# First expert chosen earlier, its w1 pieces spaced wider, and four row buffers, in a fused attention and expert kernel

## The chip, the cores and the metric

The kernel runs on one core of one Trainium2 chip. The metric is the device time of one execution in microseconds; lower is better. Engines are named as in the profile: PE (matrix multiply), PEld (its weight loads), DVE (vector), ACT (scalar), POOL (GpSimd), SP (the engine that only issues DMAs here).

## The reference

Attention over 4 batches, 8 heads, 768 tokens of 64 numbers, where a query sees only keys in the same hash bucket, and then a mixture of 8 experts in which each token goes to one expert:

```python
mask = q_bucket[:, :, :, None] == k_bucket[:, :, None, :]
scores = np.where(mask, scale * (q @ k.T), -1e9)
attn = softmax(scores);  x = (attn @ v)        # 3072 tokens x 512
e_idx = np.argmax(x @ w_gate, axis=1)
for e in range(8):
    rows = e_idx == e
    h = np.maximum(x[rows] @ w1[e], 0.0)       # 512 -> 1024
    out[rows] = gate_w * eom * (h @ w2[e])     # 1024 -> 512
```

## The kernel before

**Attention.** 16 pairs of heads, 12 steps each, 192 steps in all; a step is 128 queries against 768 keys. `scores(s)` multiplies on PE into `ps_s` (two buffers) and DVE moves the result to `sc` (L532). `soft(s)` takes the exponential on ACT (L540). `normal(s)` runs at every even step for the two steps before: DVE finishes the row sums (`rsum`, L547, L548) and POOL scales `sc` (L550). `transposed(s)` follows four steps after `scores(s)`: PE transposes (L561) and ACT copies the result to `pts` (L562). `weighted` multiplies by V (L572) into `ps_a`. Between pairs, `spread` copies the next pair's operands across partitions with DMAs issued by SP (L503 to L511).

**Work put into the steps.** `plan(step, fn)` hangs a function on a step; it is written into every engine's program there. PE, DVE, ACT and POOL run their programs in the order written; SP's order comes from the framework's scheduler. Batch b's routing is planned in the steps of the next batch: `best`, `choose`, `prefix`, `ranks` (step 144 + 20 for the third batch), `columns`, `hot`, `table`, `entries` (step 144 + 29). The last batch's routing comes after step 195 with the first expert's first product between its parts.

**The first expert.** It is chosen by load after three batches. `pick` (planned at `late`) finds it on DVE and SP reads its number (L757). `early_gather` fetches its first 256 rows from `x_dram`, an indirect DMA on POOL (L253) into `xg`. `early_turn(a)` transposes 128 of them. `early_load(cc)` loads one of the four 512 KB pieces of its w1 into `w_raw` (two buffers), and `early_w1(cc)` splits the piece into a high and a low part on POOL (L174, L177: two operations on 128 x 1024). After the last step `w2_piece(..., "hl")` does the same with the four pieces of w2, in the same two buffers. `fill(f)` are the eight blocks of the first product, `low()` the DVE operation that belongs to each (L322).

**After attention.** `gid0` holds the first expert's first 256 rows over all four batches; `gather` fetches them (`xg`, at most `EARLY` = 2 buffers). `order()` sorts the experts, `indices` makes the row numbers `gid` and `sid`. Then the early rows' second product runs (`down_rows`, in blocks of two f), and `turn` transposes the two gathered chunks between its blocks. Then come the experts in order, r = 0 to 7. `up` is a first product in pairs of f into `ps_s`, followed by `hh` on ACT (L321) and `hl` on DVE (L322). For r = 0 the next expert's rows are gathered inside the loop over `fp` and transposed where `TURN_UP` and `TURN_DOWN` say (chunks 0 and 1 after fp = 2, chunk 2 after fp = 3, chunk 3 in the second product). Later experts' rows come in quarters by `gather_part` (L285). `send` scales a finished chunk on ACT into `yo` (L327, two buffers) and stores it by an indirect DMA on POOL (L328).

Of the kernel before, what the change touches and what calls it, by code (L numbers as in the profile page):

```python
# [8 lines left out]
F32 = mybir.dt.float32  # L9
# [10 lines left out]
B, H, S, D = 4, 8, 768, 64  # L20
# [4 lines left out]
DM = H * D  # L25
E = 8
F = 1024
NTOK = B * S
NTT = NTOK // P
CH = P  # L30
NCH = 4
# [4 lines left out]
EARLY = 2  # L36
# [17 lines left out]
def f32(ap):  # L54
    return ap.bitcast(F32)
# [3 lines left out]
def lsh_attention_then_moe(  # L59
# [120 lines left out]
    def w1_load(r, cc):  # L180
        return load_weights([P, F], w1[bass.ds(expert[r], 1), :, cc].rearrange("e p f -> p (e f)"))

    def w1_split(pool, raw, idle=""):
        return split_weights(pool, "w1", NCC, [P, F], raw, idle)
# [47 lines left out]
    gp = ctx.enter_context(tc.tile_pool(name="gp", bufs=1))  # L232
# [8 lines left out]
    def indices(pool, tacc):  # L241
        gid = pool.tile([CH, E, NCH], U32, name="gid")
        nc.vector.tensor_copy(gid, tacc[:, 0])
        sk = pool.tile([CH, E, NCH], F32, name="sk")
        nc.vector.tensor_scalar(sk, tacc[:, 2], -SKIP, SKIP, ALU.mult, ALU.add)
        sid = pool.tile([CH, E, NCH], U32, name="sid")
        nc.vector.tensor_tensor(sid, sk, tacc[:, 0], ALU.add)
        return gid, sid

    def gather(idx, n=CH, ntok=NTOK, pool=gp, bufs=EARLY):  # L250

        xg = pool.tile([CH, DM], F32, name="xg", bufs=bufs)
        nc.gpsimd.indirect_dma_start(out=xg[0:n], out_offset=None, in_=x_dram[0:ntok, :],  # L253
                                     in_offset=bass.IndirectOffsetOnAxis(ap=idx[0:n], axis=0))
        return xg, n

    def new_x0():
        return [gp.tile([P, NCC, CAP0], F32R, name=n) for n in ("xh0", "xlo0")]

    def turn(xgn, xs, c0, early=False):  # L260

        xg, n = xgn
        px = (ps_m if early else ps_t).tile([P, NCC, CH], F32, name="ps_m" if early else "ps_t")
        for cc in range(NCC):
            nc.tensor.transpose(px[:, cc, 0:n], xg[0:n].rearrange("n (p b) -> n b p", b=NCC)[:, cc], ident[0:n, 0:n])
        xh, xlo = (x[:, :, c0:c0 + n] for x in xs)
        nc.scalar.copy(xh, px[:, :, 0:n])
        nc.vector.tensor_tensor(xlo, px[:, :, 0:n], f32(xh), ALU.subtract)
# [32 lines left out]
    def new_h():  # L301
        return [ep.tile([P, NFB, CAP], F32R, name=n) for n in ("hh", "hl")]
# [20 lines left out]

    def send(r, a, n, py, sid):

        yo = mp.tile([CH, DM], F32, name="yo", bufs=2)
        nc.scalar.activation(yo[0:n], py[0:n], AF.Copy, scale=tacc[0:n, 1, r, a:a + 1])  # L327
        nc.gpsimd.indirect_dma_start(  # L328
            out=out[:, :], out_offset=bass.IndirectOffsetOnAxis(ap=sid[0:n, r, a:a + 1], axis=0),
            in_=yo[0:n], in_offset=None, bounds_check=NTOK - 1, oob_is_err=False)  # L330
# [36 lines left out]
    with ExitStack() as actx:  # L367
# [16 lines left out]
        def plan(step, *fns):  # L384
            at.setdefault(step, []).extend(fns)
# [350 lines left out]
        for b in range(B - 1):  # L736
            r = routing(b)
# [7 lines left out]
        r = routing(B - 1)  # L745
# [5 lines left out]

        late = 12 * (H // 2) * (B - 1) + 29

        def load_expert(idi, i):
            expert.append(nc.values_load(idi[0:1, i:i + 1], engines=(mybir.EngineType.SP,), min_val=0, max_val=E - 1))  # L757
# [61 lines left out]
        def early_turn(a):  # L819
            if a == 0:  # L820
                early["x"] = new_x0()
            turn(early["xg"][a], early["x"], a * CH, True)

        def early_load(cc):
            early.setdefault("raw", []).append(w1_load(0, cc))

        def early_w1(cc):
            early.setdefault("w1", []).append(w1_split(wpool, early["raw"][cc], "hl"))

        plan(late, pick)  # L830
        plan(late + 2, early_gather)
        for a in range(EARLY):
            plan(late + 6 + 2 * a, lambda a=a: early_turn(a))
        for cc in range(NCC):
            plan(late + 9 + 3 * cc, lambda cc=cc: early_w1(cc))
            plan(late + (3 + cc if cc < 2 else 3 + 3 * cc), lambda cc=cc: early_load(cc))

        with tc.manual_schedule(engines=MANUAL):
            load(0)
# [86 lines left out]
    mp = ctx.enter_context(tc.tile_pool(name="mp", bufs=1, reuse_waits="tile"))  # L926
    with tc.manual_schedule(engines=MANUAL):
        xg = [gather(gid0[:, a:a + 1]) for a in range(EARLY)]
        order()
        gid, sid = indices(mp, tacc)  # L930
        x0 = new_x0()
        for c in range(EARLY):
            py = ps_s.tile([P, 2, 512], F32, name="ps_s")[:, 0]
            for f in range(0, NFB, 2):
                down_rows(c, CH, w2s, hs, py, [f, f + 1])
                if c and f < 2 * EARLY:
                    turn(xg[f // 2], x0, f // 2 * CH)
            send(0, c, CH, py, sid)
        hs = new_h()
        w1s = early["w1"]  # L940
        xs = x0
        back = None
        xgs = {}
        parts = []
        for r in range(E):
            n = CAPS[r] if r else CAP0
            ch = chunks(r)
            nxt = chunks(r + 1) if r + 1 < E else []
            if r:
                hs = new_h()  # L950
                w2s = []
            xn, w1n, splits = new_x() if nxt else None, [], []

            def fetch(a, e):

                if e < E and a < len(chunks(e)):
                    n = chunks(e)[a]
                    for k in range((n + 31) // 32):
                        parts.append((e, a, n, k))

            def gather_some(m):
                for e, a, n, k in parts[:m]:
                    if k == 0:
                        xgs[e, a] = mp.tile([P, DM], F32, name="xq", bufs=NCH), n
                    gather_part(xgs[e, a][0], idx[:, k, e, a:a + 1], k)
                del parts[:m]

            def turned(a):
                if a < len(nxt):
                    if r == 0:  # L970
                        turn(xgs.pop((r + 1, a)), xn, a * CH)
                        return fetch(a, r + 2)
                    while any(p[:2] == (r + 1, a) for p in parts):
                        gather_some(1)
                    splits.append((a, turn_blocks(xgs.pop((r + 1, a)), xn, a * CH)))

            def split():
                while splits:
                    a, fn = splits.pop(0)
                    fn()  # L980
                    fetch(a, r + 2)

            def next_w1(cc):
                if nxt:
                    w1n.append(w1_piece(wpool, r + 1, cc))

            for fp in range(NFB // 2):
                up(w1s, xs, hs, [2 * fp, 2 * fp + 1], n)()
                if r and fp < 2:
                    w2s += w2_piece(ep, r, 4 * fp) + w2_piece(ep, r, 4 * fp + 2)  # L990
                if back is not None:
                    pch = chunks(r - 1)
                    if fp < len(pch):
                        turn_back(r - 1, fp, pch[fp], back, sid)
                if r == 0 and fp == 1:
                    idx = slot_rows(tacc)
                split()
                gather_some(2)
                for a in TURN_UP.get(fp, ()):
                    turned(a)  # L1000
                if r == 0 and fp % 2 == 0:
                    for a in (fp, fp + 1):
                        if a < len(nxt):
                            xgs[1, a] = gather(gid[:, 1, a:a + 1])[0], nxt[a]

            def hook(a, cc):
                split()
                gather_some(2)
                if a is not None:
                    turned(a)  # L1010
                if cc is not None:
                    next_w1(cc)

            hooks = [lambda i=i: hook(*i) for i in TURN_DOWN]

            def between():
                if hooks:
                    hooks.pop(0)()

            if n > 3 * CH:  # L1020
                back = [mp.tile([P, 2, CAP], F32, name="yt", bufs=2) for _ in range(NCC // 2)]
                for dp in range(NCC // 2):
                    down(w2s, hs, n, back, dp, between)
            else:
                back = None
                c0 = 0 if r else EARLY
                for a in range(c0, len(ch)):
                    all_rows(r, a, a - c0, ch[a], w2s, hs, sid, between)
            split()
            if nxt:  # L1030
                w1s, xs = w1n, xn
# [98 lines left out]
```

## Time and profile before

| | |
|---|---|
| time before | 796.67 us, median of 3 runs (796.37 to 797.16) |
| the profiled execution | 791.77 us, of which the span from first to last instruction is 790.0 us |
| busy PE, PEld | 770.3 us (98%), 608.1 us (77%) |
| busy DVE, ACT, POOL | 479.7 us (61%), 459.1 us (58%), 382.1 us (48%) |
| granted clock | 0.995 on average |

The profile is one execution. Rows of the timeline give the start in us, the duration in us, the engine, the line, the operation and the tiles; in brackets stands the idle time of the engine before the row and what ended it. Rows of the waits give the waiting engine and tile, what it waited for, and the total us, the number of times and the longest. A row of the windows gives a stretch, its length, the busy us of each engine with the number of instructions, the granted PE clock, and the DMA engines' share and GB/s. The attention steps end at about 463 us, the last batch's routing at about 488 us, and the expert loop runs from about 499 us to the end.

### The profile page before, as it was taken

Reading aid. Unit: us, or ns where it says so; the run is one execution under the profiler, and the core shown is the slowest. Engines: PE = TensorE matmul, PEld = TensorE weight load, DVE = VectorE, ACT = ScalarE, POOL = GpSimd, SP = SyncE. Lnnn points to the kernel's source line nnn. Section 1 sums busy time; section 2 is a strip of 40 time slices with the busy share of each in tenths; the row PEclk is TensorE's granted clock in tenths of the full one; section 3 lists DMA queues with packets and bytes.
Section 4 is the critical chain, followed back from the end, with each engine's and each line's share of the span. In section 5 each row is a group of like instructions: output and inputs, shape, how many; then the busy total and the mean of one; then the engine's idle time right before and its main releaser. Section 6 shows DMA issues by size and latency. Waiting matters only on the chain. (4 is left out here: it accounts for less than half of the span.)

```text
span 790.0 us, 13715 instructions
## 1 busy us (share of the span) xinstructions
PE 770.3 (98%) x4690; PEld 608.1 (77%) x4690; DVE 479.7 (61%) x1032; ACT 459.1 (58%) x934; POOL 382.1 (48%) x422
## 2 busy tenths in 40 slices
PE   7999999999999999999999999999999999999997
PEld 6777676667676767676767658878999999988895
DVE  6676667796766896675896737236363636454640
ACT  6877777777777777777768721234151525353331
POOL 7555544444543444544445892372627273746201
PEclk9999999999999999999999999999999999999999
DMA  5554454464565456455456152363444444445601
GB/s 170 135 135 88 101 128 86 118 140 85 120 145 130 81 126 143 91 123 129 88 123 166 54 137 62 106 217 124 144 147 150 152 150 148 150 150 179 220 24 39
DMA packets 84800, 98.90 MB, mean 125 GB/s; under 512 B 57999, under 2 KB 59439, under 8 KB 84720
## 3 DMA queue, kind: packets, MB, share of 16 engines
q1 hardware_dynamic: 79376, 84.58, 41.1%
q0 software_dynamic: 5200, 13.31, 5.1%
q8 instruction: 40, 0.66, 0.3%
q14 instruction: 40, 0.33, 0.1%
q10 hardware_dynamic: 144, 0.02, 0.0%
HBM read 59.49 MB, written 13.11 MB: 92 GB/s over the span
## 5 line engine op out<-in xcount | busy, mean ns | idle before, releaser
L550 POOL TENSOR_SCALAR sc<-sc,rsum 128x768 f32<-128x768 f32 x192 | 178.9, 945 | 218.1 <-DVE rsum L548 85.8
L532 DVE TENSOR_SCALAR_CACHE_REDUCE sc<-ps_s 128x768 f32<-128x768 f32 x192 | 183.3, 955 | 96.4 <-PE ps_s L528 88.4
L562 ACT COPY pts<-ps_t 128x384 f32<-128x384 f32 x384 | 164.4, 481 | 95.5 <-PE ps_t L561 95.0
L540 ACT ACTIVATE sc<-sc,mn 128x768 f32<-128x768 f32 x192 | 181.4, 945 | 15.2 <-DVE sc L532 14.3
L561 PE MATMUL ps_t<-ident,sc 128*128 128x128 f32 x1152 | 158.4, 273 | 3.9 <-POOL sc L550 1.8
L561 PEld LDWEIGHTS ps_t<-ident,sc 128*128 128x128 f32 x1152 | 137.2, 141 | 14.3 <-POOL sc L550 4.6
L572 PE MATMUL ps_a<-pts,vt 128*64 128x384 f32 x768 | 144.8, 499 | 0.0
L528 PE MATMUL ps_s<-xr,xl 128*128 128x384 f32 x384 | 117.1, 386 | 2.4 <-POOL xl L476 2.2
L528 PEld LDWEIGHTS ps_s<-xr,xl 128*128 128x128 f32 x384 | 57.9, 190 | 71.0 <-issue 33.6
L528 PE MATMUL ps_s<-yr,yl 76*128 76x384 f32 x384 | 100.0, 341 | 0.6 <-POOL yr L438 0.5
L322 DVE SCALAR_TENSOR_TENSOR hl<-ps_s,hh 128x256 fp32r<-128x256 f32 (+8 forms) x40 | 34.0, 849 | 109.0 <-ACT hh L321 88.3
L311 PE MATMUL ps_s<-xh,w1h 128*128 128x256 f32 (+7 forms) x288 | 97.8, 340 | 2.2 <-DVE hl L322 2.1
L311 PE MATMUL ps_s<-xh,w1l 128*128 128x256 f32 (+7 forms) x288 | 96.2, 334 | 0.8 <-DVE w1l L177 0.5
L311 PE MATMUL ps_s<-xlo,w1h 128*128 128x256 f32 (+7 forms) x288 | 96.0, 333 | 0.0
L285 POOL DMA_INDIRECT xq<-x_dram,idx x75 | 82.5, 1099 | 21.6 <-issue 21.1
L328 POOL DMA_INDIRECT out_dram<-yo,sid x29 | 30.6, 1056 | 116.4 <-ACT yo L327 69.2
L572 PEld LDWEIGHTS ps_a<-pts,vt 128*64 128x64 f32 x768 | 46.7, 136 | 50.4 <-issue 47.7
L321 ACT ACTIVATE hh<-ps_s 128x256 fp32r<-128x256 f32 (+8 forms) x40 | 29.1, 727 | 90.4 <-PE ps_s L311 75.6
L528 PEld LDWEIGHTS ps_s<-yr,yl 76*128 76x128 f32 x384 | 70.4, 190 | 1.2 <-POOL yr L438 1.2
L311 PEld LDWEIGHTS ps_s<-xh,w1h 128*128 128x128 f32 x288 | 54.9, 191 | 5.8 <-DVE hl L322 3.0
L311 PEld LDWEIGHTS ps_s<-xh,w1l 128*128 128x128 f32 x288 | 54.8, 190 | 2.6 <-DVE w1l L177 0.9
L311 PEld LDWEIGHTS ps_s<-xlo,w1h 128*128 128x128 f32 x288 | 54.9, 190 | 1.1
(204 smaller groups left out, 1020.6 us busy)
## 6 DMA issues: line engine op xcount, KB each, us to landing
w_raw<-in_w_dram SPq DMA_DIRECT2D x36, 512.0 KB
qk<-in_qkT_dram SPq DMA_DIRECT2D x32, 384.0 KB
xh<-in_w_dram SPq DMA_DIRECT2D x14, 512.0 KB
xlo<-in_w_dram SPq DMA_DIRECT2D x14, 512.0 KB
vt<-in_v_dram SPq DMA_DIRECT2D x16, 384.0 KB
xr<-xl SPq DMA_DIRECT2D x30, 192.0 KB
yr<-xl SPq DMA_DIRECT2D x30, 192.0 KB
xr<-yl SPq DMA_DIRECT2D x30, 192.0 KB
```

The lines of the kernel that those rows point to most:

```text
L285: nc.gpsimd.indirect_dma_start(out=xq[:, k * P:(k + 1) * P], out_offset=None, in_=x_dram.rearrange("n (a f) -> (n a) f", a=NB32), in_offse ...
L311: nc.tensor.matmul(ps, l, r, start=first and k == 0, stop=last and k == len(pairs) - 1)
L321: nc.scalar.activation(hh, ph, AF.Relu)
L322: return lambda: nc.vector.scalar_tensor_tensor(hl, ph, 0.0, f32(hh), ALU.max, ALU.subtract)
L328: nc.gpsimd.indirect_dma_start(out=out[:, :], out_offset=bass.IndirectOffsetOnAxis(ap=sid[0:n, r, a:a + 1], axis=0), in_=yo[0:n], in_offse ...
L528: nc.tensor.matmul(ss[:, n, 0:HS], l[0:k, qs], r[0:k, n * HS:(n + 1) * HS], start=first, stop=not first)
L532: nc.vector.tensor_scalar(sc, ss[:, :, 0:HS], MASKED, None, ALU.min, ALU.min, accum_out=mn)
L540: nc.scalar.activation(pr, pr, AF.Exp, bias=mn, scale=-1.0, accum_out=sums[s // GROUP][:, k:k + 1])
L550: nc.gpsimd.tensor_scalar(live[s0 + k], live[s0 + k], rs[:, k:k + 1], 0.0, ALU.mult, ALU.add)
L561: nc.tensor.transpose(tr[:, c], pr[:, (3 * h + c) * P:(3 * h + c + 1) * P], ident)
L562: nc.scalar.copy(pts[:, 3 * h:3 * h + 3, t * P:(t + 1) * P], tr)
L572: nc.tensor.matmul(st["av"][j * D:(j + 1) * D], st["v"][:, j, c], blocks[hb][j][:, c], start=(c == 0), stop=(c == NT - 1))
```

## The change

Four edits.

1. `late` goes from step 173 to step 167, so `pick` stands three steps after `ranks` of the third batch. `early_gather` and the two `early_turn` keep their steps (175, 179, 181). The four `early_w1` go from steps 182, 185, 188, 191 to 176, 180, 184, 188; the four `early_load` from 176, 177, 182, 185 to 170, 171, 177, 181.
2. `xg` gets `NCH` = 4 buffers and `yo` gets 4.
3. The second expert's first two chunks (`xg1`) are gathered right after `indices`, and its other two at fp = 0; before, two were gathered at fp = 0 and two at fp = 2.
4. In the early rows' second product, the two `turn` stand after the blocks f = 2 and f = 4 of the second chunk, not after f = 0 and f = 2.

```diff
-    def gather(idx, n=CH, ntok=NTOK, pool=gp, bufs=EARLY):
+    def gather(idx, n=CH, ntok=NTOK, pool=gp, bufs=NCH):
...
-        yo = mp.tile([CH, DM], F32, name="yo", bufs=2)
+        yo = mp.tile([CH, DM], F32, name="yo", bufs=4)
...
-        late = 12 * (H // 2) * (B - 1) + 29
+        late = 12 * (H // 2) * (B - 1) + 23
...
         plan(late, pick)
-        plan(late + 2, early_gather)
+        plan(late + 8, early_gather)
         for a in range(EARLY):
-            plan(late + 6 + 2 * a, lambda a=a: early_turn(a))
+            plan(late + 12 + 2 * a, lambda a=a: early_turn(a))
         for cc in range(NCC):
-            plan(late + 9 + 3 * cc, lambda cc=cc: early_w1(cc))
-            plan(late + (3 + cc if cc < 2 else 3 + 3 * cc), lambda cc=cc: early_load(cc))
+            plan(late + 9 + 4 * cc, lambda cc=cc: early_w1(cc))
+            plan(late + (3 + cc if cc < 2 else 2 + 4 * cc), lambda cc=cc: early_load(cc))
...
         gid, sid = indices(mp, tacc)
+        xg1 = [gather(gid[:, 1, a:a + 1]) for a in range(EARLY)]
...
-                if c and f < 2 * EARLY:
-                    turn(xg[f // 2], x0, f // 2 * CH)
+                if c and f in (2, 4):
+                    turn(xg[f // 2 - 1], x0, (f // 2 - 1) * CH)
...
-                if r == 0 and fp % 2 == 0:
-                    for a in (fp, fp + 1):
-                        if a < len(nxt):
-                            xgs[1, a] = gather(gid[:, 1, a:a + 1])[0], nxt[a]
+                if r == 0 and fp == 0:
+                    for a in range(len(nxt)):
+                        xgs[1, a] = (xg1[a] if a < EARLY else gather(gid[:, 1, a:a + 1]))[0], nxt[a]
```

## The prediction

> **What bounds the kernel now.** I read the page first, then who PE waited for, then the timelines around each of those waits, and the windows for the clock.
>
> ```profile
> span 790.0 us, 13715 instructions
> PE 770.3 (98%) x4690; PEld 608.1 (77%) x4690; DVE 479.7 (61%) x1032; ACT 459.1 (58%) x934; POOL 382.1 (48%) x422
> ```
>
> PE is busy for all but 19.7 us, so only what makes PE wait, or run slowly, can move the time. The change touches nothing before step 167 (about 397 us). Between 402 and 455 us the list of PE's waits is empty; the next two lists, for 456 to 530 us and for 530 us to the end, are the whole field of the change.
>
> ```profile
> PE ps_t L561 <- POOL sc L550: 1.5, 2, 1.2
> PE ps_t L265 <- DMA xg<-x_dram,gid: 1.3, 3, 0.5
> PE ps_m L673 <- DVE ohb L649: 1.3, 1, 1.3
> PE ps_s L311 <- DVE w1l L177: 0.5, 1, 0.5
> PE ps_s L311 <- DVE hl L322: 0.4, 1, 0.4
> ...
> PE ps_s L311 <- DVE hl L322: 1.7, 1, 1.7
> ```
>
> Six groups of waits, 6.7 us. One more loss does not show as a wait:
>
> ```profile
> 475.40:478.90 3.50, 1.73 (x19) 1.59 (x19) 3.29 (x17) 0.38 (x1) 0.32 (x1) 1.00 0.17 26
> 478.90:482.30 3.40, 3.40 (x18) 3.40 (x17) 2.75 (x17) 0.74 (x2) 0.00 (x0) 0.50 0.23 34
> ```
>
> After a stretch in which PE worked 1.73 us of 3.50, its granted clock is 0.50 for 3.4 us. PE counts as fully busy there and does half the work.
>
> **The change part by part.**
>
> *Last attention steps: gain 1.5.* The wait of 1.5 us on `sc` falls on the last pair of steps:
>
> ```profile
> 455.52 1.05 POOL L174 TENSOR_SCALAR w1h<-w_raw 128x1024 fp32r<-128x1024 f32 x1
> 458.99 1.81 POOL L550 TENSOR_SCALAR sc<-sc,rsum 128x768 f32<-128x768 f32 x2
> ```
>
> The fourth w1 split (step 191) runs from 455.52 to 458.99 and the last scaling waits behind it. After the change the fourth split is at step 188, the place that the third has now, and POOL is free when the row sums come (about 456). The scaling then starts some 3 us earlier and PE's two waits go: 1.5 us.
>
> *The one-hot of the last batch: gain 1.3.*
>
> ```profile
> 473.33 2.39 POOL L177 TENSOR_TENSOR w2l<-w_raw,w2h 128x1024 fp32r<-128x1024 f32 x1
> 473.56 2.21 DVE L642 TENSOR_SCALAR eq<-df 128x48 f32<-128x48 f32 x1
> 476.77 0.20 PE L673 MATMUL ps_m<-ohb,tri 128*128 128x48 bf16 x1 [1.33 <-DVE ohb L649]
> ```
>
> L642 works on 48 numbers and took 2.21 us: it ended with the last w2 split of POOL (473.33 + 2.39 = 475.72). So POOL holds DVE, DVE holds `ohb`, and PE stood 1.33 us. After the change the w2 splits begin 3 us earlier (POOL is free, and w_raw's buffers too, since w1's last two splits come earlier), while PE and DVE arrive 1.5 us earlier. The last split would end at about 472.7 (475.72 - 3); L642 would start at 472.05 (473.56 - 1.5) and end at 472.8 instead of 475.77. `ohb` comes 0.9 us after L642 today, so at about 473.7; PE, which began to stand at 475.44 (476.77 - 1.33), is then done at 473.9. Bounds: 0 if the w2 loads hold the splits back, 1.3 if not; I take 1.3.
>
> *The half clock: gain 1.5.* With those 1.3 us of idle time gone, PE works about 3 of the 3.5 us in which it worked 1.73. I expect no drop. Half of 3.4 us is 1.7; I take 1.5, since PE was not limited by its clock in all of it. The lower end is 0.
>
> *The gathered rows: gain 2.1, less 0.1.* A turn that waits costs more than its idle time, since PE's weight loads start anew. One turn in the early rows' second product did not wait and the next did:
>
> ```profile
> 492.88 0.40 PE L311 MATMUL ps_s<-w2h,hl 128*128 128x512 f32 x1
> 493.50 0.48 PE L311 MATMUL ps_s<-w2h,hh 128*128 128x512 f32 x1
> 494.75 0.39 PE L311 MATMUL ps_s<-w2h,hl 128*128 128x512 f32 x1
> 496.06 0.48 PE L311 MATMUL ps_s<-w2h,hh 128*128 128x512 f32 x1
> ```
>
> From the product before to the product after it is 0.62 us in the first case and 1.31 in the second: 0.7 us lost per late gather. There are three (1.3 us of idle time in the list): this one and chunks 2 and 3 of the second expert, whose gathers wait today for the turns of chunks 0 and 1. With four buffers the last two are fetched at fp = 0, two products of `up` sooner; the first pair of turns moves back by one block (493.50 to 494.75 plus one product, 1.5 us) against an idle time of at most 0.5. So 3 x 0.7 = 2.1. In return only one block now lies between the second turn and `up`, which needs its low part; I put 0.1 us on that. The two gathers put ahead of `send` on POOL delay the first store by the time of two gathers; nobody waits for those with four `yo` buffers.
>
> *The output rows: gain 1.8.*
>
> ```profile
> 721.93 1.03 POOL L328 DMA_INDIRECT out_dram<-yo,sid  x1 [0.30 <-issue]
> 724.81 0.69 ACT L327 ACTIVATE yo<-ps_m,tacc 128x512 f32<-128x512 f32 x1 [12.13 <-DMA out_dram<-yo,sid]
> 725.18 0.33 PE L311 MATMUL ps_s<-xh,w1l 128*128 128x368 f32 x1
> 727.18 0.44 PE L311 MATMUL ps_s<-xh,w1h 128*128 128x368 f32 x1 [1.67 <-DVE hl L322]
> ```
>
> ACT stood 12 us for a `yo` buffer whose store left POOL late; behind it on ACT stood `hh`, behind that `hl`, and PE missed its third `up` block. With four buffers this `yo` takes one whose store is long done, and ACT is in time. From 725.18 to 727.18 instead of about 0.2: 1.8 us.
>
> *The splits that move into steps 176 and 180: cost 0.9.*
>
> ```profile
> 420.27 1.79 POOL L550 TENSOR_SCALAR sc<-sc,rsum 128x768 f32<-128x768 f32 x2
> 424.07 1.80 POOL L550 TENSOR_SCALAR sc<-sc,rsum 128x768 f32<-128x768 f32 x2 [2.01 <-DVE rsum L548]
> 428.53 0.82 PE L561 MATMUL ps_t<-ident,sc 128*128 128x128 f32 x6
> 435.49 1.05 POOL L174 TENSOR_SCALAR w1h<-w_raw 128x1024 fp32r<-128x1024 f32 x1
> 439.43 1.79 POOL L550 TENSOR_SCALAR sc<-sc,rsum 128x768 f32<-128x768 f32 x2 [0.42 <-DVE rsum L548]
> ```
>
> Today a split sets the next scaling 3.94 us after the split's start (435.49 to 439.43). Put behind the scaling of 420.27, it moves that of 424.07 to 426.0 (420.27 + 1.79 + 3.94); its second half is ready at 427.8, and PE wants it at 428.53: 0.7 us to spare. But the split also holds DVE, so `sc` and ACT come later, and the early turns of steps 179 and 181 add an ACT and a DVE operation in just these steps. By hand I get PE late by 0.3 at step 181 and 0.6 at step 184. Ends: 0 (three splits run today without a PE wait) and 3.0 (the fourth cost 1.5, and two splits are in question). I take 0.9, nearer the three.
>
> *`pick` at step 167: 0.*
>
> ```profile
> 401.09 0.94 DVE L532 TENSOR_SCALAR_CACHE_REDUCE sc<-ps_s 128x768 f32<-128x768 f32 x1
> 404.11 0.62 PE L528 MATMUL ps_s<-xr,xl 128*128 128x384 f32 x2
> 412.85 0.16 DVE L761 SCALAR_TENSOR_TENSOR o_key<-base,expi 128x8 f32<-128x8 f32 x1
> 413.98 0.16 DVE L770 SCALAR_TENSOR_TENSOR base<-lead,base 128x8 f32<-128x8 f32 x1
> ```
>
> `pick` takes DVE 1.3 us (412.85 to 414.14) and moves into a stretch where DVE is behind. The scores that reuse the buffer freed at 402.03 start at 404.11, so 2.1 us cover 1.3. The w1 loads and SP's read of the number move with it; see the last rival.
>
> Sum: 1.5 + 1.3 + 1.5 + 2.1 + 1.8 - 0.1 - 0.9 = 7.2 us. The profiled execution would go from 791.77 to 784.6. The median of the runs is 4.9 us above that execution; I take the same 7.2 off it: **789.5 us**, 0.9% faster.
>
> **The rivals.**
>
> *The half clock stays (791.0).* The waits go, but the clock drops all the same, because the small products around 477 us do not count as work or because the drop's place is free against the kernel. For it: 0.4 us of idle time on `hl` stays there. Against it: one drop, and right behind the one stretch where PE worked under half. 789.5 + 1.5. [...]
>
> *The moved splits stall PE at full price (791.6).* Two times 1.5 instead of 0.9. Against it: the empty list from 402 to 455 us with three splits in it.
>
> *A late signal goes too (788.7).*
>
> ```profile
> 519.81 0.39 PE L311 MATMUL ps_m<-w2h,hl 128*128 128x512 f32 x1
> 525.04 0.69 ACT L327 ACTIVATE yo<-ps_m,tacc 128x512 f32<-128x512 f32 x1 [6.35 <-issue]
> 527.98 0.48 PE L311 MATMUL ps_s<-xh,w1l 128*128 128x464 f32 x1 [0.52 <-DVE w1l L177]
> ```
>
> ACT took this `yo` 4.8 us after its product ended, with no releaser shown; w1's last splits stand behind it, and PE waits for them (0.5). If it is the `yo` buffer after all, four buffers win another 0.8 (0.5 idle, at the 0.7 lost for some 0.43 idle seen above). If it is not, nothing: my value, as no DMA is named.
>
> *Slower: w1's third load gets ahead of the last copies on SP (800).*
>
> ```profile
> 416.41 0.53 SPq L503 DMA_DIRECT2D xr<-xl  x1
> 422.73 0.71 SPq L511 DMA_DIRECT2D yl<-bt  x1
> 427.74 0.60 PE L528 MATMUL ps_s<-xr,xl 128*128 128x384 f32 x2
> 453.37 0.33 SPq L167 DMA_DIRECT2D w_raw<-in_w_dram  x1
> 454.99 3.33 SPq L591 DMA_DIRECT2D x_dram<-xb  x4
> ```
>
> The third load must wait for the first split, which now ends at about 425.5 (422.06, and the 3.47 us from 455.52 to 458.99). SP's order is not the written one: at 453.37 it issued a w2 load ahead of copies to `x_dram` that are written before it. If that load stands ahead of the last pair's copies (416.41 to 423.44, 7.0 us), they run from 425.5 to 432.5, and with the same 4.3 us between the end of the copies and the scores these start at 436.8 instead of 427.74: 9.1 us lost, which outweighs 7.2, and a half clock of 1.5 behind so long a gap, 800.1 in all. It decides from 8.8 us of loss on (7.2 and the 1.6 of 0.2%). Against it: the copies are written at steps 172 and 174, the load at 177, and the first two loads followed the copies today.
>
> **How the numbers follow.** Forecast 789.5: 0.52. Half clock stays, 791.0: 0.16. Splits at full price, 791.6: 0.12. Late signal goes too, 788.7: 0.10. Slower, 800: 0.05. Little is left because new waits take the place of the old ones, within 796.67 +/- 1.6: 0.05. Chances: faster by over 0.2% (about the least that a measurement of this kernel can tell from no change; 1.6 us) 0.90, within 0.2% 0.05, slower 0.05. The range takes the late signal with the splits at no cost (789.5 - 0.8 - 0.9 = 787.8), and above the half clock and the full price of the splits together (789.5 + 1.5 + 2.1 = 793.1).
>
> **What would show it.** Right: no PE wait on `sc` L550 after 456 us, L642 under 1 us or at least `ohb` not waited for, granted clock 1.00 around 479 us, no PE wait on `xg`, no ACT wait on a store at the sixth expert. Wrong: PE waits between 420 and 440 us on `sc` or `pts`, a gap before the last pair's scores, a clock of 0.50 somewhere after 400 us, or a new wait of `up` on the low part of the first rows.

## The result and the profile after

| | before | after |
|---|---|---|
| first comparison, median | 796.67 us (796.37 to 797.16, 3 runs) | 784.27 us (782.71 to 784.55, 3 runs) |
| ratio | | 0.9866 (0.9835 to 0.9897) |
| the profiled execution, its span | 791.77 us, 790.0 us | 784.55 us, 782.8 us |
| on one later chip, median | 789.69 us (788.54 to 790.24, 9 runs) | 784.21 us (783.16 to 784.6, 5 runs) |
| ratio there | | 0.993 (0.9916 to 0.9943) |

The change makes the kernel faster, by 12.4 us in the first comparison and by 5.5 us when both ran again on another chip. The changed kernel takes the same time in both; it is the kernel before that differs by 7 us. The span of the two profiled executions fell by exactly the 7.2 us of the sum, 790.0 to 782.8, and the forecast of the time, 789.5, was 5.2 us too high, outside its range.

The head of the page of the changed kernel:

```profile
span 782.8 us, 13716 instructions
...
PE 767.5 (98%) x4690; PEld 606.8 (78%) x4690; DVE 476.8 (61%) x1032; ACT 458.6 (59%) x934; POOL 380.5 (49%) x422
```

Who PE waited for, first from 390 to 455 us, then from 455 to 530 us; from 530 us to the end its list is empty:

```profile
PE ps_t L561 <- ACT pts L562: 0.4, 1, 0.4
PE ps_t L561 <- POOL sc L550: 0.2, 1, 0.2
...
PE ps_a L311 <- issue: 1.1, 1, 1.1
PE ps_s L311 <- DVE eq L642: 0.8, 1, 0.8
PE ps_t L265 <- DMA xg<-x_dram,gid: 0.4, 1, 0.4
PE ps_t L561 <- issue: 0.3, 1, 0.3
```

The waits on `ohb`, `hl` and `w1l` are gone, those on `sc` and `xg` are down to 0.2 and 0.4 us (the prediction had none left on `xg`). New are the wait on `eq` and two rows called "issue", times for which the profile shows no releaser. The wait on `pts` is in the kernel before as well. The timeline around them (the idle time and its end in brackets):

```profile
436.57 0.87 PE L561 MATMUL ps_t<-ident,sc 128*128 128x128 f32 x6 [0.15 <-POOL sc L550]
456.37 1.79 POOL L550 TENSOR_SCALAR sc<-sc,rsum 128x768 f32<-128x768 f32 x2 [0.57 <-PE ps_t L561]
470.51 2.38 POOL L177 TENSOR_TENSOR w2l<-w_raw,w2h 128x1024 fp32r<-128x1024 f32 x1
471.67 1.28 DVE L634 TENSOR_TENSOR df<-lgt,mx 128x48 f32<-128x48 f32 x1
473.21 0.17 DVE L642 TENSOR_SCALAR eq<-df 128x48 f32<-128x48 f32 x1
473.44 0.36 PE L311 MATMUL ps_s<-xh,w1h 128*128 128x256 f32 x1 [0.78 <-DVE eq L642]
515.33 0.59 ACT L267 CAST xh<-ps_t 128x512 fp32r<-128x512 f32 x1 [2.93 <-remote]
517.41 0.40 PE L311 MATMUL ps_a<-w2l,hh 128*128 128x512 f32 x1 [1.07 <-issue]
712.08 0.69 ACT L327 ACTIVATE yo<-ps_m,tacc 128x512 f32<-128x512 f32 x1 [4.87 <-PE ps_m L311]
```

The last scaling starts at 456.37 instead of 458.99. L642, which had taken 2.21 us, takes 0.17. But POOL's last split now overlaps L634, two DVE operations earlier: it takes 1.28 us and ends at 472.95, with the split (470.51 + 2.38 = 472.89). The `hl` behind it is late and PE stands 0.78 us. ACT's `yo` of the sixth expert waits for its product and for no store.

The windows over the place of the half clock (length, busy us of PE, PEld, DVE, ACT and POOL, granted clock, DMA share, GB/s):

```profile
471.57:474.98 3.41, 2.63 (x24) 2.41 (x23) 3.24 (x10) 0.67 (x3) 1.32 (x1) 1.00 0.00 0
474.98:478.39 3.41, 3.41 (x35) 3.40 (x35) 3.24 (x23) 0.83 (x3) 0.00 (x0) 1.00 0.40 58
```

To say where the time went, I divided each profiled execution at the same PE instructions of the program (named here by their start in the trace of the kernel before) and took the us between them:

```
from - to (us)   398-437 437-461 461-474 474-477 477-482 482-500 500-505 505-513 513-540 719-729  398-784
                 splits  last sc hl, eq  ohb     clock   1st xg          2nd xg          yo
before             39.45   23.66   12.86    2.95    5.52   17.05    5.32    8.15   26.96    9.99   386.00
after              39.81   22.33   13.56    1.47    3.50   17.53    5.34    7.40   25.60    8.05   378.70
e1_same            39.45   23.65   12.75    2.95    5.56   17.05    5.32    8.14   24.38    9.79   383.14
e2_schedule        39.78   22.33   13.26    1.46    3.50   18.60    5.31    8.17   24.38   10.08   380.98
e3_yo              39.45   23.64   12.87    2.95    4.04   17.69    5.31    8.14   24.41    8.05   380.68
e4_gather          39.45   23.65   12.65    2.95    5.56   17.90    5.36    7.40   24.38    9.67   383.09
e5_after           39.81   22.33   14.21    1.47    3.50   17.92    5.34    7.40   24.38    8.05   378.51
e6_last_high       39.83   22.34   13.29    1.46    3.50   17.24    5.53    7.40   24.38    8.05   377.14
e7_no_steps        39.45   23.63   12.49    2.96    5.53   16.85    5.67    7.40   24.38    8.05   380.53
e8_turns_back      39.77   22.33   13.35    1.46    3.51   18.16    5.32    7.40   24.38    8.05   377.82
e9_xg1_late        39.84   22.34   13.52    1.46    3.50   17.39    5.31    7.40   24.38    8.05   377.30
e10_both           39.82   22.33   13.47    1.47    3.50   16.87    5.13    7.40   24.38    8.05   376.51
e11_before_last    39.45   23.66   12.94    2.60    4.27   17.72    5.32    8.23   25.17    9.93   383.38
```

The two stretches left out, 540 to 719 and 729 to 784, take 179.04 and 55.07 us in every one of them. (The first 397 us, which the change does not touch, vary by up to 1.4 us between executions.)

### The profile page after: what moved, and what is told of

The parts are those of the page before. It is cut to its first block, busy times and chain, and to the rows that moved or that the text cites. A ratio compares the mean times of both kernels' runs of the same rounds, so it can differ in the third digit from the quotient of the medians.

```text
span 782.8 us, 13716 instructions
## 1 busy us (share of the span) xinstructions
PE 767.5 (98%) x4690; PEld 606.8 (78%) x4690; DVE 476.8 (61%) x1032; ACT 458.6 (59%) x934; POOL 380.5 (49%) x422
```

## The experiments

The theory after the first comparison: the sum's mechanisms hold, and what the forecast missed is the 4.9 us that the runs of the kernel before lay above its own profile, a level of those runs. The rival: those 4.9 us are waits of the kernel that the change also takes away. The runs e1 to e4 shared one chip, where the kernel before took 789.59 us (787.79 to 792.03, 29 runs); e5 to e8 a second, with 789.69 us; e9 to e11 a third, with 789.76 us (788.01 to 793.24, 17 runs).

**e1_same**: the kernel before, unchanged.

> The kernel before, unchanged, once more. The forecast took the same 7.2 us off a median that stands 4.9 us above the profiled execution, and the result came out another 5.2 us lower. Theory 1 (the 4.9 us were something outside the kernel's waits, tied to those executions): the median now lies near the profiled 791.8 us, and between single executions stand steps of about 1.5 to 1.8 us, one half-clock stretch more or less. Theory 2 (this kernel usually loses about 5 us more than its profiled execution shows, to waits that the change removes): the median is again 796 to 797 us, and the profile shows, in an execution of that length, which waits these are.

Measured: 789.3 us (788.21 to 791.6), ratio 0.9999 (0.9986 to 1.0011). In 55 further executions of the kernel before on three chips none came near 796.37, the lowest of the first comparison. So 796.67 is a level of those three runs and not of the kernel. What raised it is not shown, nor why the changed kernel, 784.27 us in the same comparison, did not have it. Of its 12 executions the profiled one was the fastest (788.21). The late `yo` that the prediction found at 525.04 us is not there: 24.38 us from 513 to 540, against 26.96. Of this difference 1.9 us are the late `yo`; the other 0.66 are the wait on the last gathered chunk (515.31 us in the kernel before, 0.40 us), which is not there either, nor in e2 and e3.

**e2_schedule**: the first edit alone.

```diff
-        late = 12 * (H // 2) * (B - 1) + 29
+        late = 12 * (H // 2) * (B - 1) + 23
... with the steps of early_gather, early_turn, early_w1 and early_load as in the change
```

> Edit 1 alone (pick at step 167, splits at 176, 180, 184, 188). From the two traces: 3.6 to 3.9 us shorter span by the first expert's second product (wait on the last scaling 1.3 of 1.5, one-hot and its two DVE waits 1.0, half clock 1.5). Theory 1: 0.995 to 0.996 of before. Theory 2, if the hidden 5 us lie in the attention part: 0.989.

Measured: 786.45 us, ratio 0.996 (0.9944 to 0.9977), 3.1 us; the sum had 1.5 + 1.3 + 1.5 - 0.9 = 3.4 for this edit. PE's waits in this profile show what it costs:

```profile
PE ps_t L265 <- DMA xg<-x_dram,gid: 2.2, 2, 1.7
...
PE ps_s L311 <- DVE eq L642: 0.5, 1, 0.5
```

PE arrives earlier at the gathered rows, and they do not come earlier by as much: 18.60 us from 482 to 500 instead of 17.05. The second gather goes out as far ahead of PE as in e1 (5.3 us), but takes 7.0 us from its issue to its landing, where it took 5.7 in e1.

**e3_yo**: four output buffers alone.

```diff
-        yo = mp.tile([CH, DM], F32, name="yo", bufs=2)
+        yo = mp.tile([CH, DM], F32, name="yo", bufs=4)
```

> Edit 2's yo buffers alone (four for two). Theory 1: 1.8 us by the wait before the sixth expert's third block, 0.9977; with the late signal of the third yo, if that was the buffer, another 0.8 to 1.9, 0.9955. Theory 2, if the hidden 5 us are stores that leave late: 0.991 or less.

Measured: 786.98 us, ratio 0.997 (0.9958 to 0.9981), 2.4 us by the ratio. The stretch from 719 to 729 falls from 9.79 to 8.05: 1.74 us, where the sum had 1.8. The half clock is also absent in this profile, though the wait on `ohb` is there (1.3 us); the section on the hardware comes back to that.

**e4_gather**: four `xg` buffers, `xg1` and the later turns, without the rest.

```diff
-    def gather(idx, n=CH, ntok=NTOK, pool=gp, bufs=EARLY):
+    def gather(idx, n=CH, ntok=NTOK, pool=gp, bufs=NCH):
...
+        xg1 = [gather(gid[:, 1, a:a + 1]) for a in range(EARLY)]
...
-                if c and f < 2 * EARLY:
-                    turn(xg[f // 2], x0, f // 2 * CH)
+                if c and f in (2, 4):
+                    turn(xg[f // 2 - 1], x0, (f // 2 - 1) * CH)
... with the gathers at fp = 0 as in the change
```

> Edits 3 and 4 with four xg buffers, alone. Theory 1: the turns of the second expert's chunks 2 and 3 no longer wait, 1.3 us, and the first pair's wait stays or goes (0 to 0.7): 0.9975 to 0.9985. Theory 2, if the hidden 5 us are gathers that land late: 0.992 or less.

Measured: 788.12 us, ratio 0.9975 (0.9963 to 0.9988), 2.0 us by the ratio and 1.5 by the medians. Its profile does not show where they come from: 383.09 us from 398 to 784 against 383.14 in e1. The table shows two effects that cancel: chunks 2 and 3 gain 0.74 us (8.14 to 7.40), while the first two chunks lose 0.85 (17.05 to 17.90), although their turns come a block later. The second of them is late:

```profile
494.59 0.63 PE L265 MATMUL ps_t<-ident,xg 128*128 128x128 f32 x4
497.73 0.75 PE L265 MATMUL ps_t<-ident,xg 128*128 128x128 f32 x4 [1.12 <-DMA xg<-x_dram,gid]
```

**e5_after**: the changed kernel.

> The changed kernel itself, beside the kernel before on one chip. Theory 1 (the three parts add up, and the 796.67 us of the first comparison was a level of those executions): ratio 0.9905, the product of 0.996, 0.997 and 0.9975, so about 782 us where the kernel before takes 789.5. Rival (the parts help one another, and the first comparison had the right size): 0.9866, about 779 us. The late signal of PE between 511 and 518 us, seen in the first profile of the changed kernel, should be absent if it belongs to those executions, and present if the back-to-back gathers on POOL cause it.

Measured: 784.21 us, ratio 0.993 (0.9916 to 0.9943). The rival's 0.9866 is out, so the first comparison overstated the change. But the parts add up to 0.9905, and the whole gives less. PE's longest waits in this profile are that on `eq`, which was 0.5 us in e2, and that on `xg`, which was 2.2 us in e2 and 1.1 in e4:

```profile
PE ps_s L311 <- DVE eq L642: 1.4, 1, 1.4
PE ps_t L265 <- DMA xg<-x_dram,gid: 0.8, 1, 0.8
```

```profile
471.49 2.38 POOL L177 TENSOR_TENSOR w2l<-w_raw,w2h 128x1024 fp32r<-128x1024 f32 x1
471.77 0.20 DVE L632 TENSOR_REDUCE mx<-lgt 128x6 f32<-128x48 f32 x1
472.01 1.92 DVE L634 TENSOR_TENSOR df<-lgt,mx 128x48 f32<-128x48 f32 x1
474.41 0.36 PE L311 MATMUL ps_s<-xh,w1h 128*128 128x256 f32 x1 [1.43 <-DVE eq L642]
```

L634 ends at 473.93, the split at 473.87. How long it is held differs between executions: the wait on `eq` is 0.8 us in the first profile of the same kernel and 0.6 and 0.7 in e8 and e9, whose edits do not touch it. The shortfall of 0.0025 has an interval of about 0.0027 to either side, so that the parts add up is not excluded. The late signal of 515 us is absent (24.38 us from 513 to 540), so the gathers on POOL, which are the same, do not cause it by themselves.

**e6_last_high**: the changed kernel with the last w2 piece's high part on ACT.

```diff
-                w2s += w2_piece(ep, 0, f, "hl")
+                w2s += w2_piece(ep, 0, f, "l" if f == NFB - 2 else "hl")
```

> The changed kernel with the high part of the last w2 piece made on ACT, which idles there from 464.4 to 470.6 us, instead of on POOL. Theory: POOL's last split (470.51 to 472.89) holds DVE's L634, hl stands behind it, and PE waits 0.8 us on it; with 1.05 us less work on POOL the split ends about 1 us sooner and the wait goes: 0.7 us faster than the changed kernel, a tenth of a per cent. Rival: the piece's load lands no sooner than POOL came to it (about 469.3), then ACT and POOL gain nothing and hh of ACT, queued behind the copy, may come later: no change or 0.3 us slower.

Measured: 783.05 us (782.49 to 783.44), ratio 0.9917 (0.9904 to 0.9931), 1.2 us below e5 on the same chip.

```profile
469.90 1.05 ACT L176 CAST w2h<-w_raw 128x1024 fp32r<-128x1024 f32 x1 [4.68 <-DMA w_raw<-in_w_dram]
471.03 2.39 POOL L177 TENSOR_TENSOR w2l<-w_raw,w2h 128x1024 fp32r<-128x1024 f32 x1 [1.06 <-ACT w2h L176]
472.46 1.02 DVE L634 TENSOR_TENSOR df<-lgt,mx 128x48 f32<-128x48 f32 x1
473.96 0.35 PE L311 MATMUL ps_s<-xh,w1h 128*128 128x256 f32 x1 [0.56 <-DVE eq L642]
```

L634 again ends with the split (473.48 and 473.42). The wait is 0.56 us, against 1.43 in e5. That does not show a gain: e8, without this edit, has the same 0.56,

```profile
473.67 0.36 PE L311 MATMUL ps_s<-xh,w1h 128*128 128x256 f32 x1 [0.56 <-DVE eq L642]
```

and e10, with it, has 0.69 against 0.73 in e9. ACT had to wait for the load, as the rival had it. A further 0.7 us against e5 in the table (17.92 to 17.24) are gathered rows that came sooner here; nothing in this edit moves them. So the traces do not say what the timed 1.2 us are.

**e7_no_steps**: the changed kernel without its first edit.

```diff
-        late = 12 * (H // 2) * (B - 1) + 23
+        late = 12 * (H // 2) * (B - 1) + 29
... with the steps of the kernel before
```

> The changed kernel without its first edit: the steps of pick, loads, splits, gathers and turns are those of the kernel before; the gathers and the four output buffers stay. If the parts add up: 0.9945 of the kernel before, 3.2 us slower than the changed kernel, with the waits on sc (1.5) and ohb (1.3) back in the list. Rival (the steps are worth less beside the others, since the new wait on eq takes 0.8 back): 2 us slower or less.

Measured: 785.63 us, ratio 0.9953 (0.9939 to 0.9966): the product of e3 and e4, 0.9945, lies within it. So nothing speaks against the other two parts adding up, and the new steps bring 1.4 us on top of them (1.9 by the means, with an interval of about 0.9 to either side), where alone they brought 3.1. That is the rival's size. By the table between e7 and e5: `sc` 1.30, `ohb` 1.49 and the clock 2.03 are won, and 0.33 between 500 and 505; the splits 0.36, `eq` 1.72 and the first gathered pair 1.07 are lost. The half clock is in this profile:

```profile
475.09:478.50 3.41, 1.62 (x19) 1.31 (x18) 3.20 (x16) 0.38 (x1) 0.53 (x1) 1.00 0.10 15
478.50:481.91 3.41, 3.41 (x19) 3.41 (x18) 3.09 (x17) 0.38 (x1) 0.00 (x0) 0.50 0.30 45
```

**e8_turns_back**: the changed kernel with the two early turns where they were.

```diff
-                if c and f in (2, 4):
-                    turn(xg[f // 2 - 1], x0, (f // 2 - 1) * CH)
+                if c and f < 2 * EARLY:
+                    turn(xg[f // 2], x0, f // 2 * CH)
```

> The changed kernel with the turns of the first two gathered chunks at f = 0 and 2 again, as in the kernel before, instead of 2 and 4. Theory: the first gather lands as late against PE as before, so the one wait on xg of 0.4 us grows by about the block of 1.5 us that lies between: 1.5 us slower than the changed kernel, 0.2 per cent. Rival (the prediction's step: a late turn costs 0.7 us, however late): 0.7 us slower. A second rival: the list of the changed kernel shows its wait at the second turn; then nothing changes.

Measured: 783.95 us, ratio 0.9936 (0.9922 to 0.9949): no difference from e5. The wait is longer, and the stretch costs 0.24 us more (18.16 against 17.92):

```profile
493.04 0.75 PE L265 MATMUL ps_t<-ident,xg 128*128 128x128 f32 x4 [1.30 <-DMA xg<-x_dram,gid]
```

It is the second turn that waits, as the second rival had it; the first chunk is there in time at either place. The time rules out the 1.5 us (the means differ by 0.3, with an interval of about 0.8 to either side), but not the 0.7. Nor is the stretch a clean test, as the second gather took 7.5 us from issue to landing in e5 and 6.6 here.

**e9_xg1_late**: the changed kernel with the gathers of `xg1` behind the first store.

```diff
-        xg1 = [gather(gid[:, 1, a:a + 1]) for a in range(EARLY)]
...
             send(0, c, CH, py, sid)
+            if c == 0:
+                xg1 = [gather(gid[:, 1, a:a + 1]) for a in range(EARLY)]
```

> The changed kernel with the two gathers xg1 issued on POOL after the first send instead of ahead of it. Theory: the second early gather lands late (PE waits 0.83 us on xg in the changed kernel, 0.42 at that place in the kernel before) because two more gathers now share the DMA engines with it and with two w1 loads; with xg1 later the stage from the first down product to the last turn takes 7.5 us instead of 8.1, about 0.5 us off the whole (less than the interval, so the stage decides). Rival: the w1 loads on SP fill the DMA engines alone; the wait stays at 0.8.

```profile
489.40 1.03 POOL L328 DMA_INDIRECT out_dram<-yo,sid  x1 [2.11 <-ACT yo L327]
490.74 0.98 POOL L253 DMA_INDIRECT xg<-x_dram,gid  x1 [0.30 <-issue]
493.41 0.75 PE L265 MATMUL ps_t<-ident,xg 128*128 128x128 f32 x4 [0.37 <-DMA xg<-x_dram,gid]
```

Measured: 782.95 us, ratio 0.9908 (0.9886 to 0.9929). The stretch from 482 to 500 takes 17.39 us against 17.92 in e5, the 0.5 us expected, and `xg` is waited for 0.37 instead of 0.83. That fits two extra gathers delaying the second chunk, but it does not show it: the first profile of the changed kernel waits 0.44 us there without this edit, and e6, with the extra gathers in the old place, 0.18. The trace's time from issue to landing of the second gather says more. With the old steps it is 5.7, 6.0 and 5.9 us without the extra gathers right behind it (e1, e3, e11) and 7.8 and 6.7 with them (e4, e7). With the new steps it is 7.0, 7.0 and 6.5 without them (e2, e9, e10) and 7.5, 6.8 and 6.6 with them (e5, e6, e8). So with the old steps the extra gathers and a longer landing go together; with the new steps the landing is long either way, for a cause that stays open.

**e10_both**: the edits of e6 and e9 together.

> The changed kernel with both single edits: the last w2 piece's high part on ACT, and xg1 issued after the first send. If the two add up: 1.2 us from the first (784.21 to 783.05) and 0.5 from the second, so a ratio of 0.991 to the kernel before, about 782.5 us. Rival: the second edit gives nothing, 0.9917 as with the first alone.

Measured: 782.7 us (782.12 to 784.64), ratio 0.991 (0.9888 to 0.9932). No wait on `xg` is left, and the traced part is the shortest of all, 376.51 us. By the time it is not told apart from e6 or e9 alone, so that the two add up is not shown. All three medians lie below both kernels'.

**e11_before_last_high**: the edit of e6 in the kernel before, and nothing else.

> The kernel before with one edit: the high part of the last w2 piece on ACT, nothing else of the change. Theory of the prediction (POOL's split holds DVE's L642, DVE holds ohb, PE stands 1.33 us, and the half clock follows that stand): the split ends about 1 us sooner, the wait on ohb falls from 1.3 to some 0.3 us, and with it PE works over 2.4 us in each stretch of 3.41 us, so that the half clock goes too: 1.0 + 1.7 = 2.7 us, ratio 0.9966. Rival A (the half clock is free of that wait): 1.0 us, 0.9987. Rival B (L642 is slow for another reason, or the piece's load holds it): no change, 1.0.

Measured: 788.66 us, ratio 0.9987 (0.9972 to 1.0001).

```profile
471.25 1.05 ACT L176 CAST w2h<-w_raw 128x1024 fp32r<-128x1024 f32 x1 [6.45 <-DMA w_raw<-in_w_dram]
472.38 2.40 POOL L177 TENSOR_TENSOR w2l<-w_raw,w2h 128x1024 fp32r<-128x1024 f32 x1 [0.96 <-ACT w2h L176]
472.95 1.86 DVE L642 TENSOR_SCALAR eq<-df 128x48 f32<-128x48 f32 x1
475.82 0.20 PE L673 MATMUL ps_m<-ohb,tri 128*128 128x48 bf16 x1 [0.98 <-DVE ohb L649]
```

L642 follows POOL's split once more (both end at 474.8), which confirms that step of the prediction. But the load of the piece lands late: the split ends 0.9 us sooner, of which 0.7 are only this execution's lead at the first place of the table (397.3 us against 398.0), and the wait on `ohb` falls by 0.35 us instead of 1.0. The half clock is absent:

```profile
474.45:477.86 3.41, 1.99 (x21) 1.68 (x20) 3.20 (x16) 0.38 (x1) 0.33 (x1) 1.00 0.15 23
477.86:481.27 3.41, 3.41 (x28) 3.12 (x26) 3.24 (x20) 0.77 (x2) 0.00 (x0) 1.00 0.26 37
```

Five of its 12 executions have a mean granted clock of 0.999, the profiled one among them. The profiles in which one drop was seen have 0.996 or 0.997, those with two 0.994 or 0.995; none of the 55 executions of the kernel before is above 0.998. That speaks for the stand at `ohb` as what brings the drop, in part of the executions. It is a hint and no proof: the mean also holds a drop near 15 us (14.69 to 18.10 in the kernel before) that stands in nine of the first ten profiles, that nothing here touches, and that this one, by its mean of 0.999, lacks too. The timed gain has rival A's size and an interval that reaches zero; it cannot say how much of it is the clock.

## Why the prediction was right or wrong

The sign, and the span of the changed kernel (forecast some 782.8 us, measured 782.8), came out; the time did not. The step that failed is "I take the same 7.2 off it". It put the gain of a profile, 791.77 us, onto a median 4.9 us above that profile. The level of 796.67 is no property of the kernel (e1: 789.3 us; 55 executions, at most 793.24). The cause of that level stays open: no trace of such an execution exists, and the changed kernel did not have it. Had I taken the sum against the execution that it was read from, 784.6 us, I had been 0.3 us off.

The terms against the two profiles, from the first two rows of the table (before to after):

- **`sc`**: 1.5 forecast, 1.33 measured; a new stand of 0.29 us ("issue", 460.07) is in it.
- **`ohb`**: 1.3 and 1.48.
- **Half clock**: 1.5, and 2.02 (5.52 to 3.50) less 0.29 that the blocks up to 492 us give back, so 1.73. Its rival fell in all seven profiles with the new steps; but two of the six with the old steps have no drop either, so not every execution gains this.
- **Gathered rows**: 2.0, and 1.42 from chunks 2 and 3 (8.15 to 7.40, and the second of the two within 513 to 540, 0.67) less 0.19 at the first pair (with that 0.29, the 17.05 to 17.53). The 0.7 us for each late gather held for chunks 2 and 3 in these two profiles; the one of chunk 3 is not in e1, e2 and e3, so the edit wins it only sometimes. It failed for the first pair: I set the turn's later place, 1.5 us, against an idle time of at most 0.5 and took the landing as fixed. From the second gather's issue to its waiting turn it was 5.7 us before (489.81 to 495.55) and 7.1 after (486.24 to 493.39), which uses the later place up. Two more gathers behind it go with a longer landing under the old steps, and the new steps lengthen it without them (e2: 7.0). In e4, with the half clock as in e1, that pair is 0.85 us slower than in e1.
- **`yo`**: 1.8 and 1.94.
- **Moved splits**: -0.9 and -0.36. PE waited once on `sc`, 0.15 us at 436.57, where I had worked out 0.3 at step 181 and 0.6 at step 184. Today's three splits without a wait were the right rows; the rival at full price is out.
- **Not in the sum**: `eq`, -0.70 (12.86 to 13.56). I let the last split end at 472.7 and L642 start at 472.05, so that it would be free at 472.8, and looked no further up DVE's queue. The split ended at 472.89, as worked out; L634, which starts 0.83 us ahead of L642 in the trace of before (472.73 and 473.56), is held instead, and `hl` stands behind it where PE needs it.
- **Not in the sum**: the late signal. From 516 us to 540 the profile of before spent 23.83 us where e1 and nearly all others spent 21.91, and the profile of after 23.14. So 0.69 us of the 7.2 are a difference of two accidents. The rival "a late signal goes too" had the right place and the wrong cause: it goes without four buffers as well (e1).

Together -0.36 + 1.33 - 0.70 + 1.48 + 1.73 - 0.19 + 1.42 + 0.69 + 1.94 = 7.3: the agreement to a tenth of a microsecond is errors that cancel. Between e1 and e5, neither with a late signal, the same stretch gains 4.6 us; e1's profile was its fastest execution, and the medians of e5's chip differ by 5.5. So against an ordinary execution the sum of 7.2 is itself too large. Between e1 and e5 two terms make up for that and more: `eq` costs 1.46 (12.75 to 14.21), and the gathered rows bring 0.16 instead of 2.0 (0.74 at chunk 2, less 0.58 at the first pair with the 0.29 of the half clock taken out). The rival of third loads ahead of the last copies did not come: the stretch from 398 to 437 us grew by 0.36 us in all.

The missing step, as the traces show it: L634 took 1.28, 1.92 and 1.02 us (the first profile of the changed kernel, e5 and e6) and ended 0.06 us behind the split each time, while L632, a reduce inside the same split, took 0.20 (e5). In e11, with no operation on POOL beside it, L634 took 0.21:

```profile
472.05 0.21 DVE L634 TENSOR_TENSOR df<-lgt,mx 128x48 f32<-128x48 f32 x1
```

The kernel before had a sign of it too: there L634 took 0.58 us and ended 0.06 us behind POOL's L174, which runs ahead of L177 (473.31 and 473.25):

```profile
472.20 1.05 POOL L174 TENSOR_SCALAR w2h<-w_raw 128x1024 fp32r<-128x1024 f32 x1
472.73 0.58 DVE L634 TENSOR_TENSOR df<-lgt,mx 128x48 f32<-128x48 f32 x1
```

Why POOL holds L634 and L642 and not L632 is not shown.

## What to carry to other kernels

Take the sum against the execution that it was read from, and ask for a second profile before trusting its small losses: a wait that is there once is worth nothing until it is there twice. When a wait is removed, walk up the waiting engine's queue as well as down: here the blocker stayed, and the engine that came sooner met it at an earlier operation (L634, 1.28 us, where L642 had taken 2.21). When something is set to be used later because its data come late, check that the data do not come later too (here 7.1 us from issue to turn, 5.7 before).

## What the runs showed of the hardware

**The half clock comes in whole steps of 3.41 us, and here it went with how the stand fell into them.** In the kernel before, the stand at `ohb` lies nearly whole within one step (475.49 to 478.90, PE at work for 1.69 us), and the next step is halved. In e3, with the same stand of 1.3 us, the steps divide it:

```profile
473.41:476.82 3.41, 2.51 (x20) 2.12 (x18) 3.34 (x5) 1.03 (x4) 2.80 (x2) 1.00 0.00 0
476.82:480.23 3.41, 2.45 (x24) 2.35 (x25) 3.19 (x17) 0.38 (x1) 0.00 (x0) 1.00 0.31 47
480.23:483.64 3.41, 3.38 (x29) 3.17 (x28) 3.39 (x15) 0.77 (x3) 0.00 (x0) 1.00 0.09 14
```

PE worked 2.5 us in each, and the clock stayed. In e1 and the windows of e7 above it worked 1.6 us in one step, and the next was halved:

```profile
473.93:477.34 3.41, 1.59 (x18) 1.29 (x17) 3.24 (x13) 0.38 (x1) 0.97 (x1) 1.00 0.02 3
477.34:480.75 3.41, 3.41 (x19) 3.41 (x18) 2.66 (x18) 0.38 (x1) 0.00 (x0) 0.50 0.38 57
```

Of six profiles with the old steps four have the drop (5.52 to 5.56 us from 477 to 482 in the table), of seven with the new steps none (3.50 or 3.51). Each drop lasts 3.41 us; the kernel before has one near its start as well:

```profile
14.69:18.10 3.41, 3.41 (x14) 3.17 (x13) 2.88 (x7) 2.44 (x7) 2.92 (x5) 0.50 0.39 115
478.90:482.31 3.41, 3.41 (x18) 3.41 (x17) 2.75 (x17) 0.75 (x2) 0.00 (x0) 0.50 0.23 34
```

The two begin 464.2 us apart, 136 times 3.413, and so they do in e4 (14.32 and 478.54) and e7 (14.29 and 478.50); that such steps run through the whole execution is inferred from this. In the one at 478.90 the products of 256 columns come 0.21 us apart, and 0.12 behind it. Busy time alone does not decide on a drop. A window with 1.6 us of work was enough for one, but in e2 a window elsewhere with 1.73 us of work kept the full clock behind it (1.00), and so did one with 1.67 at 719.37:

```profile
490.68:494.09 3.41, 1.73 (x9) 1.17 (x8) 0.69 (x1) 0.53 (x1) 0.07 (x1) 1.00 0.65 227
494.09:497.50 3.41, 3.41 (x20) 2.89 (x20) 0.69 (x1) 0.87 (x2) 0.00 (x0) 1.00 0.04 18
```

**Twice another engine went on only microseconds after a product had ended.** In the changed kernel's first profile ACT took at 515.33 a block that PE had transposed at 508.74 (0.65 us); ACT's 2.93 us of idle time before it are put down to "remote". PE then stood 1.07 us on "issue"; in the profile of the kernel before, `yo` came 4.8 us after its product. None of the eleven later profiles shows it: all spend 21.9 us between 516 and 540. What brings it about stays open.

**A turn that waited cost more than its idle time.** In the kernel before, the loads of the turn that did not wait began 0.23 us ahead of its products (492.88 and 493.11). At the one that did, PEld stood 0.84 us and PE 0.41, and both began at 495.55; from the product ahead of it to the one behind it 0.69 us more went by:

```profile
492.88 0.67 PEld L265 LDWEIGHTS ps_t<-ident,xg 128*128 128x128 f32 x4
493.11 0.63 PE L265 MATMUL ps_t<-ident,xg 128*128 128x128 f32 x4
495.55 0.56 PEld L265 LDWEIGHTS ps_t<-ident,xg 128*128 128x128 f32 x4 [0.84 <-DMA xg<-x_dram,gid]
495.55 0.75 PE L265 MATMUL ps_t<-ident,xg 128*128 128x128 f32 x4 [0.41 <-DMA xg<-x_dram,gid]
```
